# Attention block on one core: tiles 2 and 3 of the attention result turned by DMA, and later filling of the head groups' margins in DRAM

## The chip, the core and the metric

The kernel runs on one core of a Trainium2 chip. The engines are TensorE (PE in the tables; PEld is its weight load), VectorE (DVE), ScalarE (ACT), GpSimd (POOL) and SyncE (SP), whose queue issues nearly all DMAs. The metric is the time in device microseconds of one execution. The time before is 507.06 us, the median of three runs (505.41 to 508.73).

## The reference

One pre-norm block over S = 2048 rows of D = 512, one batch, in f32:

```python
h = x + attention(layernorm(x)) @ wo            # 32 heads of 16, W = 8 keys, dilation 2
#   q, k, v = layernorm(x) @ wqkv
#   row s sees rows s, s-2, ... s-14 (those below 0 masked), softmax over the 8
out = h + (relu(layernorm(h) @ w1 + b1) ** 2) @ w2 + b2     # w1: 512 x 1792
```

## The kernel before

**Tiling.** The 2048 rows are 16 tiles of 128. Four tiles form a group (`R = 4`), and attention works on pairs of tiles (`RI = 2`): pair s is tiles 2s and 2s+1, its result is `o_t[s]`. Each product is made of three fp32r matmuls per block (high times high, high times low, low times high), so every operand of a product is cast to a high part on ACT (line 152) and a low part, source minus high part, on DVE or POOL (line 155).

**Stages.** To about 64 us, tiles 0 to 3 are projected piece by piece, eight heads (one "gp" of four) at a time. Then tiles 4 to 15 are projected (`first_phase`), while DVE and POOL work on attention; the `wo` products of tiles 0 to 3 stand among these. From about 160 us three sub-blocks u = 0, 1, 2 run the MLP of one group of tiles beside the attention results and `wo` products of the next group; the MLP of the last group ends the program.

**Order.** The program order of each engine is fixed when the kernel is built. A clock of planned times, `now["pe"]` and `now["dve"]`, does it: work is put into slots with `at`, `midway` and `after`, and at the end of a slot `pump` emits attention steps on DVE as long as `now["dve"]` is below `now["pe"]`. Whatever is added to or left out of `now["pe"]` therefore moves the attention steps against the other work on DVE, POOL, ACT and SP. Every engine executes its list in order, so an instruction that waits holds all behind it.

**Attention.** One step multiplies q by a window of keys (line 339, `pr<-qp,k`), a reduction (line 373) gives logits, softmax follows, the weights are multiplied by a window of values (line 350, `pr<-ex,v`), and POOL adds the eight products up (line 407, `pr<-pr` and last `o<-pr`). q, k and v live in DRAM in `qkv_d`: ACT evacuates a projected piece to the buffer `y2`, which has two halves (lines 521 and 523), SP stores it (lines 497 and 500), and SP loads windows of k, v and q (lines 247 and 260). Each head group has a margin of eight rows in front of its second chain, filled by `store_halo` (line 487): two DMAs from DRAM to DRAM for each gp, emitted two slots after the store of that gp's first pair of tiles. They read rows that this store writes, so SP waits there until the store has landed.

**Turning the result.** The `wo` product needs `o_t` with features on the partitions. Tiles 4 to 15 (`OV`) go by DMA: `o_split` copies the 16-bit halves apart on ACT (line 616), `turn_dma` issues a DMA transpose on SP (line 620), `o_join` copies the halves together on ACT (line 625). Tiles 0 to 3 go through PE (`o_T`: four 128x128 transposes, line 201), at the half slots `OT = 4, 5, 10, 12`, with the `wo` products at `WO = 7, 9, 13, 15`. In both ways the high and low parts `oh` and `ol` (in one buffer `ohl` for the third tile of a group) are made after it. The buffers `row(...)` come from one pool of 15 that rotates. `h_add` (line 661, `h<-wo`) adds the residual on DVE and waits for the end of a tile's `wo` product.

Of the kernel before, what the change touches and what calls it, by code (L numbers as in the profile page):

```python
# [19 lines left out]
R = 4  # L20
RI = 2
# [9 lines left out]
LAG = 3  # L31
HALF = 2.6
AS = (8, 9, 12, 13)
OV = tuple(range(4, 16))
HV = (0,1,4,5,8,9,12,13)
SLOW = 1.01, 1.08, 1.05
DELAY = 3
# [21 lines left out]
def block_kernel(ctx, tc, x, wqkv, wo, w1, b1, w2, b2, out):  # L59
# [15 lines left out]
    def chain(e, g, c, r, ap):  # L75
        block = (e * 3 + c) * G + g
        return bass.AP(tensor=qkv_d.tensor, offset=qkv_d.offset + block * CS + r * GC, ap=ap)
# [35 lines left out]
    def at(delta, fn, *a):  # L113
        due.setdefault(now["slot"] + delta, []).append((fn, a))
# [115 lines left out]

    items = [(s, g0, 2) for g0 in range(0, G, 2) for s in range(RI)]
    items += [(s, g0, 4) for s in range(RI, NS) for g0 in range(0, G, 4)]
    stored = set()
    done = {s: 0 for s in range(NS)}
    o_t = {}

# [34 lines left out]
    def attention():  # L271
# [1 line left out]
        N = len(items)  # L273

        def ready(n):
            return n < N and all((items[n][0] // RI, (items[n][1] + j) // 2) in stored
                                 for j in range(0, items[n][2], 2))

        steps = [(n, j) for n in range(N) for j in range(items[n][2])]
        ks, vs, qs, qps, ex = {}, {}, {}, {}, {}  # L280
# [203 lines left out]
    def store_halo(gp):  # L484

        for g in (2 * gp, 2 * gp + 1):
            nc.sync.dma_start(chain(0, g, 2, 0, [[G * 3 * CS, 2], [GC, PAD], [1, GC]]),
                              chain(0, g, 2, PAD, [[0, 2], [0, PAD], [1, GC]]))

    def store(t, gp, c, y):  # L490

        b, r = divmod(t, 8)
        e, i = divmod(r, 4)
        pos = PAD + CH // 2 * b + i
        if c is None:
            for j in range(2):
                nc.sync.dma_start(chain(e, 2 * gp + j, 0, pos,
                                        [[R * GC, P], [G * CS, 3], [1, RI * GC]]), y[:, :, j])
        else:
            nc.sync.dma_start(chain(e, 0, c, pos, [[R * GC, P], [CS, G], [1, RI * GC]]), y)  # L500
        if t == 0:
            at(2, store_halo, gp)
        if i == R - RI:
            if c is None:
                stored.add((t // R, gp))
            elif c == 2:
                stored.update((t // R, gp) for gp in range(G // 2))
# [84 lines left out]
    def o_T(t):  # L592
        s, j = divmod(t, RI)
        pump(until=s)
        tr = transposes(o_t[s][:, j, :])
        if t % R == RI:

            ohl = att.tile([P, 2, KB, P], F32R, name="ohl", tag="o", bufs=3)
            oT[t] = ohl[:, 0], ohl[:, 1]
        else:  # L600
            oT[t] = row("oh", (P, KB, P), F32R), row("ol", (P, KB, P), F32R)
        at(0, hi_T, tr, [oT[t][0]])
        at(0, lo_T, tr, [oT[t][0]], [oT[t][1]])
# [30 lines left out]
    def o_join(t):  # L634
        turn_join(("o", t))
        tr = planes.pop(("o", t))
        if t % R == RI:
            ohl = att.tile([P, 2, KB, P], F32R, name="ohl", tag="o", bufs=3)
            oT[t] = ohl[:, 0], ohl[:, 1]
        else:  # L640
            oT[t] = row("oh", (P, KB, P), F32R), row("ol", (P, KB, P), F32R)
        hi_T(tr, [oT[t][0]])
        (at if t >= 12 else midway)(0, lo_T, tr, [oT[t][0]], [oT[t][1]])

    def h_split(t):
        turn_split(("h", t), hn.pop(t))
# [360 lines left out]
    def first_phase(t0):  # L1007
        def chores(m):
            if t0 + 3 < 16:
                if m in (0, 2):  # L1010
                    at(0, x_stats, t0 + 2 + m // 2)

                early = t0 == 12
                if m + early in ((4, 6) if t0 == R else (6, 7)):
                    at(0, x_norm, t0 + 2 + (m + early) // 7 if t0 > R else t0 + m // 2)
                if m in XT[early]:
                    x_T(t0 + 2 + XT[early].index(m))
            if t0 + 5 < 16 and m in (6, 9):
                at(0, load_x, t0 + 2 + m // 3)
            if jobs and m % 3 == 0:  # L1020
                at(0, weight_job)
            k = t0 // 2 * 12 - 72 + m
            if k == 19:
                dve(HOLD)
            for t in range(R):
                if k == OT[t]:
                    at(0, load_h, t)
                    o_T(t)
                if t in HV and k == HK[t][0]:
                    at(0, h_split, t)  # L1030
                    after(0, turn_dma, ("h", t))
                if t in HV and k == HK[t][1]:
                    at(0, turn_join, ("h", t))
                if k == WO[t]:
                    wo_product(t, (1, 3, 4, 6))
                    now["pe"] += 2.73
                if k == HT[t]:
                    (at(0, h_parts, t) if t in HV else h_T(t))
            if k in W2:
                at(0, load_w2, W2.index(k))  # L1040

        def half(m):
            end_slot(1.37)
            chores(m)

        for n in range(6):
            chores(2 * n)
            qkv_of(t0 + n % 2, n // 2, lambda: half(2 * n + 1))
            end_slot(1.37)
# [200 lines left out]
```

## Time and profile before

| | |
|---|---|
| three runs | 505.41, 507.06, 508.73 us |
| the profiled execution | 506.54 us, of which 504.7 us are the span of its instructions |
| mean granted TensorE clock | 0.999 |
| busy: PE, PEld | 497.3 us (99%), 421.1 us (83%) |
| busy: DVE, POOL, ACT | 380.5 us (75%), 356.4 us (71%), 304.2 us (60%) |
| DMA queue of SP | 101.61 MB, 68.8% of the 16 DMA engines' span |
| DMA share from 64 to 120 us, from 120 to 140 us | 0.94, 0.75 |
| PE transposes of `o` (tiles 0 to 3) | 16 of 272 ns, 2.4 us in all |

Times in rows are microseconds from the first instruction, unless a row says ns. A row of the timeline is: start, duration, engine, line, operation, output and inputs, shapes, count, and in brackets the idle time of the engine just before, with what ended it. Matmuls overlap, so PE's durations add up to more than the time between starts; differences of starts are used for PE. The busy shares are averages: what matters for a change is which engine ends the wait at its place.

### The profile page before, as it was taken

The numbers are of one execution on the slowest core, as the hardware profiler recorded it, in microseconds if no ns is written. First come the engines' busy times: TensorE is split into PE (matmuls) and PEld (weight loads), VectorE is DVE, ScalarE is ACT, GpSimd is POOL, SyncE is SP. The second block draws the span as 40 slices with busy tenths as digits, with TensorE's granted clock in tenths as the row PEclk, the third lists the DMA queues.
The fourth block names the chain that finished last, engine by engine and source line by source line (L and its number), as shares of the span: only waits on it lengthen the run. The fifth ranks groups of instructions, "written<-read, shape, count | busy, mean of one in ns | idle before, by whom it ended". The sixth has DMA issues, their size and how long they took to land.

```text
span 504.7 us, 7544 instructions
## 1 busy us (share of the span) xinstructions
PE 497.3 (99%) x2422; PEld 421.1 (83%) x2422; DVE 380.5 (75%) x512; ACT 304.2 (60%) x558; POOL 356.4 (71%) x434
## 2 busy tenths in 40 slices
PE   8999999999999999999999999999999999999997
PEld 7999778888888888888888888778888888998986
DVE  6479799999989999788879988998972147833233
ACT  4634677768346758378464567845566937666541
POOL 5714789896685999879777876896897464685610
PEclk9999999999999999999999999999999999999999
DMA  8678899999698999679576866867672372354112
GB/s 268 200 213 201 241 306 296 267 279 306 211 219 255 302 279 260 202 215 259 161 256 213 211 199 166 210 230 257 204 169 71 98 198 83 130 159 150 64 43 83
DMA packets 109359, 102.61 MB, mean 203 GB/s; under 512 B 29448, under 2 KB 77832, under 8 KB 109320
## 3 DMA queue, kind: packets, MB, share of 16 engines
q1 hardware_dynamic: 108376, 101.61, 68.8%
q10 hardware_dynamic: 944, 0.52, 0.3%
q8 instruction: 19, 0.31, 0.2%
q14 instruction: 20, 0.16, 0.1%
HBM read 72.65 MB, written 24.25 MB: 192 GB/s over the span
## 4 chain that ended last, share of the span: by engine, by line
PE 73%; POOL 5%; ACT 5%; DVE 3%; issue 2%; DMA 1%; SPq 0%; POOLq 0%; ACTq 0%
PE mm L228 35%; PE acc L895 23%; PE wo L228 7%; PE mm L818 6%; POOL pr L407 2%; PE tr L201 2%; ACT pl L616 1%; DVE pr L350 1%; DMA h<-h_d 1%; POOL o L407 1%; POOL rl L155 1%; ACT r L872 1%; POOL h L674 1%; ACT r L871 0%; ACT hn L196 0%
## 5 line engine op out<-in xcount | busy, mean ns | idle before, releaser
L407 POOL TENSOR_TENSOR pr<-pr 128x512 f32<-128x512 f32 (+1 forms) x128 | 133.9, 1046 | 34.2 <-DVE pr L350 28.8
L228 PE MATMUL mm<-big_l,w_h 128*128 128x512 f32 x336 | 88.5, 389 | 0.1
L350 DVE TENSOR_TENSOR pr<-ex,v 128x1024 f32<-128x1024 f32 x64 | 78.0, 1220 | 12.9 <-POOL o L407 7.9
L339 DVE TENSOR_TENSOR pr<-qp,k 128x1024 f32<-128x1024 f32 x64 | 76.8, 1201 | 7.8 <-ACT qp L268 7.2
L373 DVE TENSOR_REDUCE ex<-pr 128x64 f32<-128x1024 f32 x64 | 78.5, 1226 | 1.9
L228 PEld LDWEIGHTS mm<-big_l,w_h 128*128 128x128 f32 x336 | 63.0, 188 | 13.6 <-ACT qp L268 0.5
L155 POOL TENSOR_TENSOR rl<-r,rh 128x512 fp32r<-128x512 f32 x42 | 55.2, 1316 | 20.3 <-ACT rh L152 20.2
L228 PE MATMUL mm<-big_l,xh 128*128 128x512 f32 (+1 forms) x208 | 55.8, 378 | 0.0
L228 PE MATMUL mm<-big_h,xh 128*128 128x512 f32 (+1 forms) x208 | 53.7, 379 | 0.7 <-ACT xh L152 0.7
L228 PE MATMUL mm<-big_h,xl 128*128 128x512 f32 (+1 forms) x208 | 52.7, 375 | 0.8 <-DVE xl L155 0.8
L895 PE MATMUL acc<-big_l,rh 128*128 128x512 f32 x190 | 52.2, 390 | 0.0
L895 PE MATMUL acc<-big_h,rh 128*128 128x512 f32 x190 | 52.1, 391 | 0.0
L895 PE MATMUL acc<-big_h,rl 128*128 128x512 f32 x190 | 51.7, 389 | 0.0
L228 PE MATMUL mm<-big_l,w_l 128*128 128x512 f32 x168 | 44.9, 389 | 0.0
L228 PEld LDWEIGHTS mm<-big_h,xh 128*128 128x128 f32 x208 | 37.7, 188 | 7.6 <-ACT xh L152 1.8
L228 PEld LDWEIGHTS mm<-big_h,xl 128*128 128x128 f32 x208 | 38.2, 188 | 7.0 <-DVE xl L155 1.2
L895 PEld LDWEIGHTS acc<-big_h,rl 128*128 128x128 f32 x190 | 35.7, 188 | 7.5
L895 PEld LDWEIGHTS acc<-big_l,rh 128*128 128x128 f32 x190 | 35.5, 188 | 7.4
L228 PEld LDWEIGHTS mm<-big_l,xh 128*128 128x128 f32 x208 | 37.5, 188 | 4.9
L871 ACT ACTIVATE r<-mm,b_sb 128x512 f32<-128x512 f32 x42 | 28.8, 685 | 19.8 <-PE mm L228 19.8
L895 PEld LDWEIGHTS acc<-big_h,rh 128*128 128x128 f32 x190 | 34.9, 188 | 6.7
L228 PEld LDWEIGHTS mm<-big_l,w_l 128*128 128x128 f32 x168 | 31.5, 188 | 6.6
(167 smaller groups left out, 917.5 us busy)
## 6 DMA issues: line engine op xcount, KB each, us to landing
k<-qkv_d SPq DMA_DIRECT2D x48, 288.0 KB, 3.0
v<-qkv_d SPq DMA_DIRECT2D x48, 288.0 KB, 3.2
qkv_d<-y SPq DMA_DIRECT2D x18, 512.0 KB, 4.9
big_l<-w2l_d SPq DMA_DIRECT2D x24, 256.0 KB, 3.1
xt<-in_A_x_dram SPq DMA_DIRECT2D x16, 256.0 KB, 4.7
q<-qkv_d SPq DMA_DIRECT2D x32, 128.0 KB, 3.4
h<-in_A_x_dram SPq DMA_DIRECT2D x16, 256.0 KB, 3.7
h_d<-h SPq DMA_DIRECT2D x16, 256.0 KB, 3.2
```

The lines of the kernel that those rows point to most:

```text
L155: eng.tensor_tensor(out=dst, in0=src, in1=h, op=ALU.subtract)
L201: nc.tensor.transpose(tr[:, k, :], src[:, k * P:(k + 1) * P], ident)
L228: nc.tensor.matmul(ps, l(k), r(k), start=(n == 0), stop=(n == 3 * KB - 1))
L339: nc.vector.tensor_tensor(out=pr.rearrange("p i w h d -> p i w (h d)"), in0=qps["now"][:, j % 2].unsqueeze(2).to_broadcast([P, RI, W, GC]) ...
L350: nc.vector.tensor_tensor(out=p2, in1=vwin, op=ALU.mult, in0=e1[:, :, :, j * GH:(j + 1) * GH].unsqueeze(4).to_broadcast([P, RI, W, GH, DH]))
L373: nc.vector.tensor_reduce(out=lf[:, :, :, j * GH:(j + 1) * GH], in_=pr, axis=X, op=ALU.add)
L407: nc.gpsimd.tensor_tensor(out=dst, in0=p2[:, :, :w], in1=p2[:, :, w:2 * w], op=ALU.add)
L616: nc.scalar.copy(two_planes(planes[key][1]), halves_of(src))
L674: nc.gpsimd.tensor_tensor(out=h, in0=h, in1=b2_sb, op=ALU.add)
L818: nc.tensor.matmul(ps, sta[y][:, k], mov[x][:, k], start=(first and q == 0), stop=(last and q == len(terms) - 1), skip_group_check=True)
L871: nc.scalar.activation(r, ps, AF.Relu, bias=b1_sb[:, f:f + 1])
L895: nc.tensor.matmul(acc[j], l[:, j * P:(j + 1) * P], w[f], start=(first and n < len(js)), stop=(last and n >= len(terms) - len(js)))
```

## The change

`OV` now holds tiles 2 and 3 too: they are turned as tiles 4 to 15 are. `OK` gives the half slots: split at 6 and 8, join at 11 and 13; the transposes on PE at 10 and 12 are gone. The `wo` products stay at 13 and 15; for tiles in `OV` they take the term with the low part last. Second, `store_halo` is put four slots behind the store and no longer two (for the first gp it stays in the second slot, but behind what that slot holds already), and attention may start on a gp only when its margin has been issued (`padded`).

```diff
-OV = tuple(range(4, 16))
+OV = tuple(range(2, 16))
+OK = {2: (6, 11), 3: (8, 13)}
...
-            return n < N and all((items[n][0] // RI, (items[n][1] + j) // 2) in stored
-                                 for j in range(0, items[n][2], 2))
+            gps = [(items[n][1] + j) // 2 for j in range(0, items[n][2], 2)] if n < N else []
+            return n < N and all((items[n][0] // RI, gp) in stored and gp in padded
+                                 for gp in gps)
...
+        padded.add(gp)
...
         if t == 0:
-            at(2, store_halo, gp)
+            if gp:
+                at(4, store_halo, gp)
+            else:
+                at(2, at, 0, at, 0, store_halo, gp)
...
-        (at if t >= 12 else midway)(0, lo_T, tr, [oT[t][0]], [oT[t][1]])
+        (at if t >= 12 or t < R else midway)(0, lo_T, tr, [oT[t][0]], [oT[t][1]])
...
                 if k == OT[t]:
                     at(0, load_h, t)
-                    o_T(t)
+                    if t not in OV:
+                        o_T(t)
+                if t in OK and k == OK[t][0]:
+                    at(0, o_split, t)
+                    after(0, turn_dma, ("o", t))
+                if t in OK and k == OK[t][1]:
+                    at(0, o_join, t)
```

Line numbers of the changed kernel are larger by 1 to 6 for the same code (line 487 is 489 there, 497 is 500, 661 is 667).

The order on SP from the fifth store to the last margin, before:

```order
L497 DMA qkv_d<-y_90 128x3x128 x2
L260 DMA q<-qkv_d 128x2x128
L487 DMA qkv_d<-qkv_d 2x8x64 x2
L497 DMA qkv_d<-y_90 128x3x128 x4
L247 DMA k<-qkv_d 128x704
L260 DMA q<-qkv_d 128x2x128
L487 DMA qkv_d<-qkv_d 2x8x64 x2
L438 DMA xt<-in_A_x_dram 128x512
L497 DMA qkv_d<-y_90 128x3x128 x2
```

The same stretch with the change:

```order
L500 DMA qkv_d<-y_90 128x3x128 x2
L261 DMA q<-qkv_d 128x2x128
L500 DMA qkv_d<-y_90 128x3x128 x2
L489 DMA qkv_d<-qkv_d 2x8x64 x2
L500 DMA qkv_d<-y_90 128x3x128 x2
L248 DMA k<-qkv_d 128x704
L261 DMA q<-qkv_d 128x2x128
L440 DMA xt<-in_A_x_dram 128x512
L500 DMA qkv_d<-y_90 128x3x128 x2
```

The margin of the second gp (`qkv_d<-qkv_d`) stands one store later; that of the third has left this stretch and stands behind the load of `b_sb`; that of the fourth stands behind `raw<-in_A_wo_dram` and one more store, where it stood ahead of both.

ACT around the turning of tile 2, with the change (before, the three rows with `pl<-o` are not there and the cast of `ohl` reads `tr`, the result of PE):

```order
L622 COPY pl<-o 128x1024
L153 CAST xh<-tr 128x512
L269 COPY qp<-q 128x256
L529 COPY y_90<-mm 128x8x64
L153 CAST xh<-tr 128x512
L622 COPY pl<-o 128x1024
L153 CAST w_h<-raw 128x448
L529 COPY y_90<-mm 128x8x64
L197 ACTIVATE hn<-h,rs 128x512
L631 COPY pl<-o 128x1024
L153 CAST ohl<-pl 128x512
L153 CAST w_h<-raw 128x448
```

The splits of tiles 2 and 3 (line 622) and the join of tile 2 (line 631) are new; the join of tile 3 follows a little later, ahead of the cast of its `oh`. `hn<-h,rs` now stands ahead of the cast of `ohl`, where it stood behind it.

DVE in sub-block u = 0, around the residual additions of tiles 4 and 5, before:

```order
L373 TENSOR_REDUCE ex<-pr 128x16x4
L661 TENSOR_TENSOR h<-wo,h 128x512
L163 BN_STATS st<-h 128x6
L164 BN_AGGR mv<-st 128x2
L339 TENSOR_TENSOR pr<-qp,k 128x1024
L350 TENSOR_TENSOR pr<-ex,v 128x1024
L373 TENSOR_REDUCE ex<-pr 128x16x4
L155 TENSOR_TENSOR ol<-pl,oh 128x512
L350 TENSOR_TENSOR pr<-ex,v 128x1024
L661 TENSOR_TENSOR h<-wo,h 128x512
```

And with the change:

```order
L667 TENSOR_TENSOR h<-wo,h 128x512
L164 BN_STATS st<-h 128x6
L165 BN_AGGR mv<-st 128x2
L375 TENSOR_REDUCE ex<-pr 128x16x4
L341 TENSOR_TENSOR pr<-qp,k 128x1024
L352 TENSOR_TENSOR pr<-ex,v 128x1024
L156 TENSOR_TENSOR ol<-pl,oh 128x512
L375 TENSOR_REDUCE ex<-pr 128x16x4
L667 TENSOR_TENSOR h<-wo,h 128x512
L164 BN_STATS st<-h 128x6
L165 BN_AGGR mv<-st 128x2
L352 TENSOR_TENSOR pr<-ex,v 128x1024
```

One attention step that stood ahead of each `h<-wo,h` now stands behind it. The same has happened in u = 1 at tile 8: before, `ex<-pr`, `ol<-pl,oh`, `pr<-qp,k`, `h<-wo,h`, `pr<-ex,v`; now `ol<-pl,oh`, `ex<-pr`, `h<-wo,h`, `pr<-qp,k`, `pr<-ex,v`. The PE transposes that are left out no longer add their 2 times 0.44 us to `now["pe"]`.

More of the change, by code (lines that the diff above doesn't have):

```diff
@@ L232, in block_kernel @@
     items += [(s, g0, 4) for s in range(RI, NS) for g0 in range(0, G, 4)]
-    stored = set()
+    stored, padded = set(), set()
     done = {s: 0 for s in range(NS)}
```

## The prediction

> **What bounds the kernel now.** I read the share of each engine first, then PE's waits, then the places of those waits.
>
> ```profile
> span 504.7 us, 7544 instructions
> PE 497.3 (99%) x2422; PEld 421.1 (83%) x2422; DVE 380.5 (75%) x512; ACT 304.2 (60%) x558; POOL 356.4 (71%) x434
> PE wo L228 <- ACT ohl L152: 0.8, 1, 0.8
> PE mm L228 <- DVE xl L155: 0.8, 1, 0.8
> ```
>
> The first two lines are the head of the page, the others are from the table of PE's waits (total, times, longest). PE is without work for only 7.4 us of the span, so a gain has two sources: fewer matmuls, or one of those waits. The reverse weighs more: DVE, POOL and ACT have spare time on average, but each executes in order, and wherever one of them delivers late to PE, that time is lost in full. The profiled execution took 506.54 us; I add terms to that. It lies 0.5 us below the median of 507.06, less than the runs differ among themselves, so I forecast the median by the same number.
>
> **Term 1: the transposes on PE.** PE's timeline at tile 2:
>
> ```profile
> 134.99 0.60 PE L201 MATMUL tr<-ident,o 128*128 128x128 f32 x4
> 135.34 1.17 PE L228 MATMUL mm<-big_h,xh 128*128 128x512 f32 x4
> 136.35 1.08 PE L228 MATMUL mm<-big_l,xh 128*128 128x512 f32 x4
> 137.27 1.07 PE L228 MATMUL mm<-big_h,xl 128*128 128x512 f32 x4
> ```
>
> Four matmuls of 512 columns take 137.27 - 136.35 = 0.92 us; with the transposes ahead of them, 136.35 - 134.99 = 1.36. So a turning costs PE 0.44 us net, and PE has no wait here: two of them gone are **-0.9**, with little doubt.
>
> What takes their place is paid elsewhere. The groups of instructions, split by shape, and the list of DMAs (median us to landing):
>
> ```profile
> L616 ACT COPY pl<-o 128x1024 uint16<-128x1024 uint16 x12 | 12.5, 1043 | 8.3 <-POOL o L407 8.3
> L625 ACT COPY pl<-o 128x1024 uint16<-128x1024 uint16 x12 | 14.0, 1170 | 1.4 <-DMA o<-pl 1.3
> L155 DVE TENSOR_TENSOR ohl<-pl,ohl 128x512 fp32r<-128x512 f32 x3 | 4.0, 1325 | 7.7 <-ACT ohl L152 7.7
> L155 DVE TENSOR_TENSOR ohl<-tr,ohl 128x512 fp32r<-128x512 f32 x1 | 0.7, 657 | 0.0
> L155 DVE TENSOR_TENSOR ol<-pl,oh 128x512 fp32r<-128x512 f32 x9 | 7.9, 883 | 0.0
> L155 DVE TENSOR_TENSOR ol<-tr,oh 128x512 fp32r<-128x512 f32 x3 | 2.1, 688 | 2.4 <-ACT oh L152 2.4
> o<-pl SPq DMA_TRANSPOSE x12, 3.8
> ```
>
> ACT gets two splits and two joins, 2 x (1.04 + 1.17) = 4.4 us, and DVE's low parts cost (1.33 - 0.66) + (0.88 - 0.69) = 0.9 us more. The landing of 3.8 us does not count. ACT's row ahead of the new split is
>
> ```profile
> 123.80 0.82 ACT L196 ACTIVATE xt<-xt,rs 128x512 f32<-128x512 f32 x1
> ```
>
> so tile 2's split ends near 125.7, and its join, five half slots of about 2.3 us later, comes near 136.4. SP gets two issues, ahead of a k load and of a weight load; the loads run two steps ahead and DMA has a share of 0.75 here (table above), so I take nothing, with 0 to 0.7 us as bounds (one issue held back).
>
> The low parts read `tr` from PSUM before, and now two operands in SBUF. The rows show the effect: 657 ns against 1325, 688 against 883. The Trainium skill (SBUF — State Buffer, "SBUF: two separate sides") says that a VectorE operation with two SBUF inputs and a GpSimd operation that reads SBUF lock each other out for a whole instruction. By that rule the difference is chance by chance up to one POOL operation, and not a fixed price; the means of the rows agree with it, and the second rival below is what it would do at its worst.
>
> **Term 2: the margins.** SP, ACT, DVE and PE, one after the other:
>
> ```profile
> 37.42 1.23 SPq L487 DMA_DIRECT2D qkv_d<-qkv_d  x2
> 49.63 1.24 SPq L487 DMA_DIRECT2D qkv_d<-qkv_d  x2
> 51.86 0.89 SPq L497 DMA_DIRECT2D qkv_d<-y  x2
> 50.22 0.59 ACT L523 COPY y<-mm 128x512 f32<-128x512 f32 x1 [3.26 <-DMA qkv_d<-y]
> 56.13 0.58 ACT L523 COPY y<-mm 128x512 f32<-128x512 f32 x1 [1.22 <-DMA qkv_d<-y]
> 57.63 0.29 DVE L362 TENSOR_REDUCE sm<-ex 128x16 f32<-128x128 f32 x1 [2.40 <-ACT ex L396]
> 63.10 0.68 DVE L155 TENSOR_TENSOR xl<-tr,xh 128x512 fp32r<-128x512 f32 x1
> 63.83 0.96 PE L228 MATMUL mm<-big_h,xl 128*128 128x512 f32 x3 [0.77 <-DVE xl L155]
> ```
>
> The fourth gp's margin waits on SP to 49.63, and behind it stands the store of 51.86, whose landing ACT waits for at 56.13. ACT executes in order, so the softmax behind that evacuation is late, DVE waits 2.40 us for it, and the low part at 63.10 makes PE wait 0.77. With the margins behind the stores, this store goes out as soon as its data are there, some 4 us earlier, and ACT loses at least the 1.22. DVE has no other wait between 57.63 and 63.10 that could take up 0.77 us. **-0.77**; bounds -0.8 and 0 (the softmax found late for another reason). SP now waits for the last margin with v loads behind it, but from about 48 rather than 49.63.
>
> **Term 3: the start of u = 0.** The joins come late on an ACT that DVE waits for anyway:
>
> ```profile
> 140.44 0.69 DVE L155 TENSOR_TENSOR ol<-tr,oh 128x512 fp32r<-128x512 f32 x1 [1.74 <-ACT oh L152]
> 161.39 0.74 DVE L155 TENSOR_TENSOR big_l<-tr,big_l 128x256 fp32r<-128x256 f32 x2
> 163.21 1.98 PE L228 MATMUL mm<-big_l,w_h 128*128 128x512 f32 x8
> ```
>
> Following ACT's new list (evacuation, `hn`, join, cast of `ohl`) I get `ohl` ready near 138.2, where DVE took it at 136.91, and tile 3's `oh` near 142.6. DVE, almost without other gaps to 160, is then about 1.1 us later. Against this, one reduction of 1.2 us now stands behind the first MLP low parts and not ahead. Their end stays near 162.1; PE, 0.9 us earlier by term 1, wants the last at 163.21 - 0.9 = 162.3. I take **+0.1**, bounds 0 and 0.7.
>
> **Term 4: tile 6 in u = 0.** With 0.88 less on PE's planned clock, each attention step falls behind the residual addition that it stood ahead of (order of DVE, above). That addition waits for PE:
>
> ```profile
> 205.15 0.69 DVE L661 TENSOR_TENSOR h<-wo,h 128x512 f32<-128x512 f32 x1 [1.63 <-PE wo L228]
> 209.11 2.44 POOL L407 TENSOR_TENSOR pr<-pr 128x512 f32<-128x512 f32 x2 [1.62 <-DVE pr L350]
> 218.57 1.05 ACT L616 COPY pl<-o 128x1024 uint16<-128x1024 uint16 x1 [1.73 <-POOL o L407]
> 228.49 0.62 ACT L152 CAST ohl<-pl 128x512 fp32r<-128x512 f32 x1
> 229.43 0.84 PE L228 MATMUL wo<-wo_h,ohl 128*128 128x512 f32 x3
> ```
>
> The reduction ran in PE's shadow before 205.15; now it is executed after it, so the next product with v, and POOL's sum that waits for it at 209.11, are 1.15 us later. POOL has no gap to the last `o`, ACT waits for that to split tile 6 at 218.57, and ACT has no gap from there to the cast that ends at 229.11. PE takes it at 229.43: slack 0.32. All this hangs on PE's own clock through the `wo` at 205.15, so term 1 changes nothing. 1.15 - 0.32 gives **+0.8**; bounds 0 (the softmax or a copy elsewhere gives the step back) and 1.2.
>
> **Term 5: tile 10 in u = 1.** The same at tile 8:
>
> ```profile
> 293.40 0.69 DVE L661 TENSOR_TENSOR h<-wo,h 128x512 f32<-128x512 f32 x1 [0.61 <-PE wo L228]
> 299.29 2.48 POOL L407 TENSOR_TENSOR pr<-pr 128x512 f32<-128x512 f32 x2 [1.34 <-DVE pr L350]
> 307.37 1.05 ACT L616 COPY pl<-o 128x1024 uint16<-128x1024 uint16 x1 [2.07 <-POOL o L407]
> 317.95 0.62 ACT L152 CAST ohl<-pl 128x512 fp32r<-128x512 f32 x1
> 318.62 1.21 PE L228 MATMUL wo<-wo_h,ohl 128*128 128x512 f32 x4 [0.78 <-ACT ohl L152]
> ```
>
> Here the multiplication with k, 1.2 us, falls behind the wait. The sum at 299.29 comes 1.2 to 1.3 us later, POOL then has no gap to the `o` at 307.34, ACT none from there to 318.57, and PE waits already. The stall of 0.78 becomes about 2.0: **+1.2**, bounds -0.8 (the order helps and the stall goes) and 1.5.
>
> **Term 6: u = 2.**
>
> ```profile
> 396.89 0.62 ACT L152 CAST ohl<-pl 128x512 fp32r<-128x512 f32 x1
> 401.74 1.07 PE L228 MATMUL wo<-wo_h,ohl 128*128 128x512 f32 x4
> ```
>
> The cast is 4.2 us ahead of PE, more than one step: **0**.
>
> **The sum.** -0.9 - 0.77 + 0.1 + 0.8 + 1.2 + 0 = +0.43, so 506.54 + 0.43 = **507.0 us**. The change gives PE 1.7 us and takes about 2 back through the order of DVE. A difference of 1% (5 us) is about what a measurement of this kernel can tell from no change, so this is no change that a few runs would show.
>
> **The rivals.**
>
> *The gains stay.* The step's delay is absorbed: DVE, POOL and ACT wait in all for 1.6 to 2.1 us on that chain (rows of terms 4 and 5), and if POOL's or ACT's list is favourable, the split goes out as before. For it: in both chains the waiting engine idles just ahead of the split. Against it: it idles because the one before it is late, which the step makes worse. Price: terms 3 to 5 fall away: 506.54 - 1.67 = 504.9 us. If the stall of 0.78 goes too, 504.1. Chance 0.25.
>
> *VectorE becomes the bound at the start of u = 0* (slower). Mechanism: the two new low parts read two SBUF operands and are held by POOL each time. For `ohl<-pl` the trace has one of 1.81 us:
>
> ```profile
> 318.60 1.81 DVE L155 TENSOR_TENSOR ohl<-pl,ohl 128x512 fp32r<-128x512 f32 x1 [0.58 <-ACT ohl L152]
> ```
>
> If both low parts take that long, DVE loses (1.81 - 1.33) + (1.81 - 0.88) = 1.4 us more than in term 3, and if `oh` is also late by one held copy of 1.05 us on ACT, about 2.5. It decides as soon as the last MLP low part ends after 162.3 on PE's clock; beyond that PE loses it one to one, since DVE and PE stay busy with no gap there. 507.0 + 2.5 = 509.5 us. Against it: the mean of the group is 883 and 1325 ns, and that is in term 3. Chance 0.2.
>
> *The margins do nothing for PE.* ACT's evacuation at 56.13 is freed, but the softmax is late by another load that SP now holds behind the last margin; the stall at 63.83 stays. 507.0 + 0.77 = 507.8 us. Speaks against it that SP's waits in this stretch all get shorter. Chance 0.1.
>
> There is a rule against the first half of the change as such: the Trainium skill (VectorE: DVE Perf Modes, "The three transpose paths" and "Rules for kernel authors") gives 390 ns for a 128x128 transpose on TensorE and 1309 by DMA, and advises TensorE where PSUM will do as its target. By latency the rule would keep PE; as the landing is hidden here (11 us from split to join) it changes no term, and the sum by it would only lose the -0.9, 507.9.
>
> **How the numbers follow.** Forecast 0.45, gains stay 0.25, VectorE bound 0.2, margins idle 0.1. The likeliest case gives the prediction, 507.0. The range reaches from the full gain with some scatter of runs, 504.2, to the slower rival, 509.6; each side leaves out about one in ten (the bounds of terms 3 to 5 at their worst together give 506.54 - 1.67 + 3.4 = 508.3, inside). Over 1% faster would need below 502, more than PE's waits and both gains give together: 0.03. Over 1% slower, beyond 512, needs the slower rival twice over: 0.07.
>
> **What would show it.** Right: 8 fewer transposes, no wait of PE near 63, waits of PE for `ohl` of about 0.8 us at tile 6 (near 228) and of about 2 at tile 10 (near 317). Term 3 is wrong if PE waits near 161 for a `big_l` low part. Terms 4 and 5 are wrong if the splits of tiles 6 and 10 lie no later against PE than before. All of it is wrong if PE shows waits of over 3 us in sum at places not named here, above all for k, v or the evacuation of projections between 120 and 160.

## The result and the profile after

The changed kernel takes **508.79 us** (median of 22 runs, 507.18 to 510.97), the kernel before 507.0 us beside it on the same chip (22 runs, 505.41 to 508.73). The ratio is 1.0038, with an interval of 1.0029 to 1.0046: slower by 0.4%. The forecast was 507.0 us, which is no change, in a range of 504.2 to 509.6. The time lies in the range, but the 1.8 us that the change costs were not forecast.

The profiled execution took 508.45 us. Of its page the head, and of the table of PE's waits (total, times, longest):

```profile
span 506.6 us, 7539 instructions
PE 497.0 (98%) x2414; PEld 420.5 (83%) x2414; DVE 377.9 (75%) x512; ACT 308.9 (61%) x562; POOL 356.2 (70%) x434
PE wo L229 <- ACT ohl L153: 2.7, 2, 1.9
PE mm L229 <- DVE xl L156: 0.8, 1, 0.8
PE mm L229 <- ACT r L877: 0.5, 1, 0.5
PE mm L229 <- DVE big_l L156: 0.2, 1, 0.2
```

PE has the 8 transposes less (2422 to 2414) and ACT the 4 copies more. The wait for `xl` that the margins were to take away is still there, the wait for `ohl` went from 0.8 to 2.7 us, and two waits are new. PE's timeline shows where they lie:

```profile
63.79 0.73 PE L229 MATMUL mm<-big_h,xl 128*128 128x512 f32 x2 [0.77 <-DVE xl L156]
160.71 1.16 PE L229 MATMUL mm<-big_l,w_h 128*128 128x512 f32 x4 [0.18 <-DVE big_l L156]
169.64 1.19 PE L229 MATMUL mm<-big_l,w_h 128*128 128x512 f32 x4 [0.50 <-ACT r L877]
230.50 0.73 PE L229 MATMUL wo<-wo_h,ohl 128*128 128x512 f32 x2 [0.72 <-ACT ohl L153]
321.05 0.73 PE L229 MATMUL wo<-wo_h,ohl 128*128 128x512 f32 x2 [1.93 <-ACT ohl L153]
```

**Stretches.** To place the time I cut each span at instructions of PE that all kernels have (a transpose of `xt` or `hn`, a `wo` product) and took the differences of their starts in PE's timeline. In the table "start" ends at the fourth transpose of `xt`; "margins" is the stretch from 59 to 74 us, "turning" the one from 129 to 156 (the first transpose of `hn`), "u=0" from the next transpose of `hn`, 3.2 us later, to the first `wo` product of tile 4, "tile 6" and "tile 10" the stretches between the `wo` products of tiles 5 and 6, and 9 and 10, "u=2" from the end of u = 1 to the `wo` product of tile 12. The stretches left out differ by 0.25 us at most, but for two in e8_all_early, which the text on it names.

```
                  start  margins  turning    u=0  tile 6  tile 10    u=2   span
before            14.42    15.15    27.29  42.68   17.22    18.17  43.00  504.7
after             14.38    15.16    26.33  43.88   18.11    19.32  42.62  506.6
e1_halo_only      14.39    14.58    27.30  42.65   17.23    18.18  43.01  504.1
e2_halo_pinned    14.41    14.09    27.30  42.65   17.23    18.16  43.01  503.6
e3_turn_only      15.84    14.55    26.31  43.92   18.21    19.37  42.63  507.7
e4_order_only     14.14    14.63    27.30  42.64   18.10    19.32  42.63  505.7
e5_turn_paid      14.55    16.21    26.32  43.57   17.41    18.18  43.01  506.3
e6_all_paid       14.85    14.88    26.31  43.57   17.37    18.18  43.04  505.2
e7_all_pinned     14.81    14.08    26.32  43.53   17.41    18.18  43.04  504.3
e8_all_early      14.32    14.08    26.32  46.13   17.23    17.22  42.68  508.0
e9_one_ahead      15.81    14.07    27.29  42.63   17.23    17.22  43.59  504.5
e10_joins_early   14.36    14.09    26.33  44.31   17.23    18.20  43.61  504.8
e11_best          14.38    14.09    26.33  44.49   17.23    17.22  43.62  503.9
e12_one_turn      14.49    14.08    26.62  42.63   17.23    18.18  43.01  503.0
```

After against before: turning -0.96, u=0 +1.20, tile 6 +0.89 (and +0.14 right behind), tile 10 +1.15, u=2 -0.38, margins nothing; that makes +2.0 of the 1.9 us between the spans, and the medians differ by 1.8. Between kernels with the same code in a stretch its time agrees to some 0.05 us, 0.10 at most (tile 6 in after and e3_turn_only), except in "start" and "margins": before, e3, e4 and e5 have the same code there, and one execution of each took 14.55 to 16.21 us in "margins". So I compare stretches, and the ratios only as a second witness. A wait costs PE more than its idle time: where an old wait grew, at tile 10, the loss is the growth (0.78 to 1.93, 1.15), but at tile 6 a new wait of 0.72 cost 0.89, and in u=0 two new ones of 0.18 and 0.50 cost 1.20, about 0.2 to 0.3 more for each new wait.

### The profile page after: what moved, and what is told of

Same layout as the page of the kernel before. It is cut to its first block, busy times and chain, and to the rows that moved or that the text cites. A ratio compares the mean times of both kernels' runs of the same rounds, so it can differ in the third digit from the quotient of the medians.

```text
span 506.6 us, 7539 instructions
## 1 busy us (share of the span) xinstructions
PE 497.0 (98%) x2414; PEld 420.5 (83%) x2414; DVE 377.9 (75%) x512; ACT 308.9 (61%) x562; POOL 356.2 (70%) x434
## 4 chain that ended last, share of the span: by engine, by line
PE 47%; POOL 8%; ACT 6%; DVE 4%; issue 2%; DMA 1%; SPq 0%; POOLq 0%; ACTq 0%; DVEq 0%
PE acc L901 21%; PE mm L229 15%; PE mm L824 6%; PE wo L229 4%; POOL pr L409 3%; POOL rl L156 1%; ACT pl L622 1%; DMA raw<-in_B_w_dram 1%; ACT r L877 1%; DVE pr L341 1%; POOL o L409 1%; DVE pr L352 1%; POOL h L680 1%; ACT r L878 1%; ACT hn L197 1%
```

## The experiments

Ratios are against the kernel before on the same chip.

**The margins alone.** The edit is the diff's part on `store_halo` and `padded`; tiles 2 and 3 stay on PE.

> Only the margins are put later; tiles 2 and 3 stay on PE. Theory: ACT's evacuation near 56 comes 1.6 us earlier, but the multiplication with k on DVE that started at 54.00 now waits for POOL to about 56.4, because the build gives it the buffer that POOL still reads; the wait of PE near 63.8 stays at 0.77 and the profiled execution takes 506.5 us as before (median within 0.3 of the kernel before). Rival (the buffer plays no part, the gain was lost through the turned tiles): the wait near 63.8 is gone, 505.7 us.

Measured: 506.27 us (12 runs), ratio 0.9995 (0.9985 to 1.0005): no difference. Its margins stretch has 14.58 where before has 15.15, but with unchanged margins it was also 14.55 and 14.63 in two other kernels below. The theory's wait of DVE for POOL is there; its other half, that PE's wait near 63.8 stays at 0.77, did not hold in this execution: POOL was 0.6 us earlier than in the change, and PE's product began at 63.17, without a listed wait. DVE in this stretch, first before, then the margins alone, then the whole change:

```profile
54.00 1.22 DVE L339 TENSOR_TENSOR pr<-qp,k 128x1024 f32<-128x1024 f32 x1 [0.19 <-ACT qp L268]
```

```profile
55.83 1.22 DVE L340 TENSOR_TENSOR pr<-qp,k 128x1024 f32<-128x1024 f32 x1 [1.69 <-POOL o L408]
```

```profile
56.45 1.22 DVE L341 TENSOR_TENSOR pr<-qp,k 128x1024 f32<-128x1024 f32 x1 [3.04 <-POOL o L409]
57.59 0.28 DVE L364 TENSOR_REDUCE sm<-ex 128x16 f32<-128x128 f32 x1
```

ACT and POOL of the whole change at the same place:

```profile
54.54 0.58 ACT L529 COPY y<-mm 128x512 f32<-128x512 f32 x1
55.73 0.26 ACT L398 ACTIVATE ex<-ex 128x128 f32<-128x128 f32 x1
```

```profile
55.96 0.46 POOL L409 TENSOR_TENSOR o<-pr 128x128 f32<-128x128 f32 x1
```

What the prediction followed did happen: the evacuation started at 54.54, where it stood at 56.13 before, and the softmax behind it ended at 55.99. But DVE did not use it. Its multiplication `pr<-qp,k`, which started at 54.00 before, now waited until POOL had finished reading a product at 56.42, and the reduction `sm<-ex` behind it started at 57.59, where it was at 57.63 before. One wait took the place of the other, to 0.04 us. The order of DVE's list had not changed here; its waits had. These are two multiplications with k that stand four instructions apart on DVE (59 and 63 are their places in its list, and the brackets name the engines they wait for), before and after:

```
59 L339 TENSOR_TENSOR pr<-qp,k 128x1024 [waits Activation_49]
63 L339 TENSOR_TENSOR pr<-qp,k 128x1024 [waits Pool_49]

59 L341 TENSOR_TENSOR pr<-qp,k 128x1024 [waits Activation_49,Pool_49]
63 L341 TENSOR_TENSOR pr<-qp,k 128x1024
```

The products `pr` share three buffers that the build hands out. With the margins moved, the first of these two products was given a buffer that POOL still reads, and the second one that DVE's own reduction frees; before it was the other way round.

**The same with the buffers named.** To test this I gave the `pr` buffers by name, in the sequence of before. The few other tiles that share these three buffers are named too; the order of DVE's list is that of the margins alone. The first of the edited lines:

```diff
-pr = att.tile([P, RI, W, GH, DH], F32, name="pr", bufs=3)
+pr = att.tile([P, RI, W, GH, DH], F32, name="pr", tag="pr" + next(turns), bufs=1)
```

> As e1, but each product buffer is named by hand in the sequence that the kernel before had, so the multiplication with k does not wait for POOL. Theory: it starts at about 54.1, the softmax is there at 55.7, PE's wait near 63.8 is gone: 0.8 us under the kernel before, profiled 505.7 us. Rival (POOL's sum or the loads are late in any case): PE's wait stays, 506.5 us.

Measured: 505.57 us (10 runs), ratio 0.9982 (0.9967 to 0.9997). DVE in this stretch:

```profile
53.51 1.22 DVE L342 TENSOR_TENSOR pr<-qp,k 128x1024 f32<-128x1024 f32 x1
55.05 0.29 DVE L365 TENSOR_REDUCE sm<-ex 128x16 f32<-128x128 f32 x1 [0.32 <-ACT ex L399]
```

No wait for POOL, the softmax's reduction is 2.6 us earlier than in before, and PE has no wait near 63. The stretch takes 14.09 us; it took 14.07 to 14.09 in each of the seven kernels with moved margins and named buffers, 14.58 to 15.16 with moved margins and the build's choice (three kernels), and 14.55 to 16.21 with the margins of before (four). So the margins are worth 0.5 to 2.1 us when the buffer stays, and the buffer took it away in the change.

**The turning alone.** The diff's part on `OV`, `OK` and the copies; margins as before.

> Only tiles 2 and 3 are turned by DMA; the margins stay where they were. Theory (the order on DVE costs the time): PE waits 0.7 for ohl near 230, 1.9 near 320, 0.5 for r near 169, as with the whole change; -0.9 + 0.7 + 1.1 + 0.5 + 0.2 = +1.6, profiled 508.1 us. Rival (the later margins cost it, by the DMA queue): at most 505.7 us.

Measured: 510.49 us (6 runs), ratio 1.0078 (1.0059 to 1.0097). The stretches from turning on repeat those of the whole change (26.31, 43.92, 18.21, 19.37), and its waits too. So the loss belongs to this half. The median is 3.7 us above before, of which these stretches explain 2.2; the profiled run shows a start that was 1.4 us longer, and the other runs aren't seen.

**The order alone.** The kernel before, turning on PE, but with the 0.44 taken off the planned clock at tiles 2 and 3, so that POOL's list is that of the change, and DVE's too, but for the low part of tile 3, which stands ahead of a product with v and not behind it:

```diff
+                    if t in (2, 3):
+                        now["pe"] -= 0.44
```

> The kernel before, with tiles 2 and 3 on PE, but 0.44 taken off PE's planned clock at each of their two transposes, so that DVE and POOL get exactly the order of the changed kernel. Theory (the order alone costs the time): PE waits near 169, 230 and 320 as with the change, 506.5 + 0.7 + 1.1 + 0.5 = 508.8 us or a little more. Rival (ACT's four copies, the two transposes on SP and the DMA load cost it): 506.5 us, PE waits only 0.8 near 319.

Measured: 509.12 us (6 runs), ratio 1.0061 (1.0043 to 1.0079); the profiled run, at 507.49, is the lowest of them. PE's timeline:

```profile
229.47 1.19 PE L228 MATMUL wo<-wo_h,ohl 128*128 128x512 f32 x4 [0.71 <-ACT ohl L152]
320.03 1.19 PE L228 MATMUL wo<-wo_h,ohl 128*128 128x512 f32 x4 [1.93 <-ACT ohl L152]
```

Without a single DMA turning more, tile 6 and tile 10 lose what they lose in the change (18.10, 19.32). So terms 4 and 5 are the shifted step alone. The stretch u=0 loses nothing (42.64), though a wait near 169 was expected: its loss needs the turning.

**The turning with its order paid back.** The turning alone, and where PE's transposes are left out the planned clock still gets their 0.44; DVE's list is then that of before, but for the same low part:

```diff
                     if t not in OV:
                         o_T(t)
+                    else:
+                        now["pe"] += 0.44
```

> Only tiles 2 and 3 are turned by DMA, and PE's planned clock still gets 0.44 at the two places of the transposes, so that DVE and POOL keep the order of the kernel before. Theory: the waits near 169 and 230 are gone, the one near 320 is back at 0.8; the 0.9 us of the transposes stay, profiled 505.6 us. Rival (PE, now 0.9 us earlier, runs into weights and low parts that are not earlier, at the start of u = 0): 0.5 to 1.2 us are lost there again, 506.1 to 506.8 us.

Measured: 507.36 us (12 runs), ratio 1.0001 (0.9984 to 1.0018). Tile 6 and tile 10 are back (17.41, 18.18), turning has its 0.97 less, and u=0 has 0.89 more, by one wait, as the rival said:

```profile
162.41 1.15 PE L229 MATMUL mm<-big_l,w_h 128*128 128x512 f32 x4 [0.62 <-ACT y L526]
```

The bracket names an evacuation on ACT; what this product does wait for is worked out at the end of this section. So the turning by itself, without the shifted order, is worth -0.97 + 0.89 + 0.19 (tile 6): about nothing.

**The whole change, paid back; and with the buffers named.** Two kernels: the change with the same two lines, and that one with `pr` named as above.

> The whole change with PE's planned clock paid as in e5. Theory: as e5, and as e1 showed for the margins with the changed buffers, 0 to 0.5 us less: 505.1 to 505.6 us. Rival (margins and turned tiles disturb each other on SP): over 506.5 us.

Measured: 507.35 us (12 runs), ratio 1.0006 (0.9985 to 1.0028). The time is the rival's, but its cause doesn't show: the stretches are those of the turning paid back, and the theory had counted on the 0.97 that u=0 takes back.

> As e6, with the product buffers named by hand as in e2. Theory: the gains add up, 1.0 of e2 and 0.9 of the transposes: 504.6 us; it beats both kernels. Rival (the start of u = 0 gives the 0.9 back): 505.5 us.

Measured: 506.06 us (12 runs), ratio 0.9972 (0.9957 to 0.9986). With the order and the buffer of before, the change gains about 0.3%; its stretches differ from those of the margins with named buffers only by -0.98 in turning, +0.88 in u=0 and +0.18 at tile 6, so its gain is that of the margins. The start of u = 0 gives the 0.9 back, as the rival said.

**The step pushed the other way.** The last kernel with 0.88 in place of 0.44, so that each step comes earlier than in before:

> As e7, but 0.88 instead of 0.44 is added at the two places, so that attention steps move one step ahead of the order before. Theory (each step ahead of a residual addition takes its time out of PE's wait): PE's wait for tile 10's ohl near 317, 0.8 in all kernels with the old order, gets smaller or goes, 503.8 to 504.3 us. Rival (the step now stands ahead of the MLP's low parts at 161): a wait of about 1 us there, 505.5 us.

Measured: 508.22 us (12 runs), ratio 1.0027 (1.0004 to 1.005). Tile 10 loses its wait (17.22), as the theory said, and the rival's wait near 161 came too; neither had the rest. u=0 takes 46.13, with PE waiting there three times:

```profile
160.31 1.15 PE L229 MATMUL mm<-big_l,w_h 128*128 128x512 f32 x4 [0.90 <-DVE big_l L156]
162.81 2.14 PE L229 MATMUL mm<-big_l,w_h 128*128 128x512 f32 x8 [0.45 <-DVE big_l L156]
170.77 1.20 PE L229 MATMUL mm<-big_l,w_h 128*128 128x512 f32 x4 [1.28 <-ACT r L882]
340.57 0.66 PE L202 MATMUL tr<-ident,hn 128*128 128x128 f32 x4 [2.24 <-ACT hn L197]
```

The fourth, at the end of u = 1, lies in a stretch left out of the table (4.23 us there, 1.82 in before; the other is the one behind tile 10's, 17.07 for 16.54). So the sign of the step isn't a rule: each stall has its own place.

**One step earlier in u = 1 only.** The margins with named buffers, turning on PE, and the planned clock 0.88 ahead from slot 0 to slot 12 of u = 1:

```diff
+            if u == 1 and p in (0, 12):
+                now["pe"] += 0.88 if p == 0 else -0.88
```

> As e2 (margins later, buffers named by hand, tiles 2 and 3 on PE), and only in the first part of u = 1 PE's planned clock is 0.88 ahead, taken back behind the split of tile 10. In DVE's order three pairs change: each of the residual additions of tiles 8 and 9 falls behind one multiplication with v, and the low part of tile 9 behind a reduction. Theory (the place of one step against an addition that waits for PE sets when POOL, ACT and then PE get on): the opposite move to that of the change, so PE's wait of 0.8 for tile 10's ohl goes, the stretch from tile 9's product to tile 10's takes 17.3 us in place of 18.2, 502.7 us. Rival (tile 10's wait has another source, such as the landing of its transpose): 18.2 us stay, 503.6 us.

Measured: 504.98 us (12 runs, 504.63 to 506.65), ratio 0.9963 (0.9949 to 0.9976): the fastest kernel of this study that computes the whole, ahead of before and of the change. The wait at tile 10 is gone (17.22 for 18.16), and a wait that was not expected stands at the start of u = 2 (+0.58), so that 0.58 of the 0.94 won is lost again:

```profile
338.87 1.15 PE L228 MATMUL mm<-big_l,w_h 128*128 128x512 f32 x4 [0.71 <-DVE big_l L155]
```

**The joins one half slot earlier.** The whole change, paid and with named buffers, and the joins at 10 and 12:

```diff
-OK = {2: (6, 11), 3: (8, 13)}
+OK = {2: (6, 10), 3: (8, 12)}
```

> As e7, but the joins of tiles 2 and 3 stand one half slot earlier (10 and 12). Theory (the joins and casts on ACT make DVE late, by its waits of 0.6 and 1.4 us for the casts near 137 and 142): DVE's waits shrink, its low parts at 160 end up to 1 us earlier, and the start of u = 0 takes 42.7 to 43.0 us in place of 43.5. Rival (PE is earlier than DVE there by the 0.97 of the transposes alone, whatever the joins do): 43.5 us stay.

Measured: 506.42 us (12 runs), ratio 0.9991 (0.9978 to 1.0004). The stretch u=0 got worse, 44.31, against what either theory expected, and u=2 is 0.57 longer, with a wait of 0.7 for `big_l`. DVE's low parts of the two turned tiles, and the product with v beside the second, with the joins as in the change and then one half slot earlier:

```profile
137.53 0.69 DVE L156 TENSOR_TENSOR ohl<-pl,ohl 128x512 fp32r<-128x512 f32 x1 [0.62 <-ACT ohl L153]
139.27 1.22 DVE L354 TENSOR_TENSOR pr<-ex,v 128x1024 f32<-128x1024 f32 x1
141.91 0.69 DVE L156 TENSOR_TENSOR ol<-pl,oh 128x512 fp32r<-128x512 f32 x1 [1.42 <-issue]
```

```profile
136.40 0.69 DVE L156 TENSOR_TENSOR ohl<-pl,ohl 128x512 fp32r<-128x512 f32 x1
140.79 0.69 DVE L156 TENSOR_TENSOR ol<-pl,oh 128x512 fp32r<-128x512 f32 x1 [2.56 <-ACT oh L153]
141.40 1.22 DVE L354 TENSOR_TENSOR pr<-ex,v 128x1024 f32<-128x1024 f32 x1
```

DVE lost the wait for `ohl` and got one of 2.56 us for `oh`. The edit had changed DVE's order as well, at this one place: the low part of `oh` now stands ahead of a product with v of 1.2 us, and no longer behind it. So DVE came to it before ACT had made `oh`, and these waits together grew from 2.04 to 2.56 us. Why PE lost so much by it, the last part of this section shows.

**Both.** The last kernel with the step of u = 1 put ahead:

> e9 and e10 together on the whole change: margins later, buffers named by hand, tiles 2 and 3 by DMA with PE's planned clock paid and the joins earlier, 0.88 ahead in the first part of u = 1. Theory: the gains add up, 0.9 less than e10 in tile 10's stretch; it beats the kernel before by 2.5 to 3.5 us. Rival: the turned tiles give back what they gain, no better than e9.

Measured: 505.93 us (12 runs), ratio 0.998 (0.9967 to 0.9992). Tile 10 has no wait, u=0 takes 44.49; it is no better than the step alone with turning on PE, as the rival said.

**What u=0 waits for.** These kernels give a rule for the start of u = 0. As a mark I take the first `h<-wo` on DVE after 129 us. In before, the mark is at 130.82, and the pair of low parts that PE's first MLP product needs (`big_l<-tr`) and that product are

```profile
159.60 0.74 DVE L155 TENSOR_TENSOR big_l<-tr,big_l 128x256 fp32r<-128x256 f32 x2
161.38 1.09 PE L228 MATMUL mm<-big_l,w_h 128*128 128x512 f32 x4
```

In the whole change, the mark and the pair are

```profile
130.77 0.68 DVE L667 TENSOR_TENSOR h<-wo,h 128x512 f32<-128x512 f32 x1
159.82 0.74 DVE L156 TENSOR_TENSOR big_l<-tr,big_l 128x256 fp32r<-128x256 f32 x2
```

The same places in the other kernels; where PE waits, its product starts 0.89 us after the pair starts. This holds in e7 and e10 too, where the profile's bracket names a work of ACT for the wait; in the program this product has no wait for that work, but one for the pair.

```
                  DVE's pair after the mark    PE's product after the mark    PE's wait
before                    28.78                       30.56                      -
after                     29.05                       29.94                     0.18
e3_turn_only              29.06                       29.95                     0.20
e7_all_pinned             29.47                       30.36                     0.62
e8_all_early              29.75                       30.64                     0.90
e10_joins_early           30.06                       30.95                     1.20
```

Take the wait off, and PE reaches the product 29.74 to 29.76 us after the mark in all five turned kernels, 0.8 us earlier than before. In before PE could have started at 28.78 + 0.89 = 29.67 and did at 30.56: 0.89 us to spare (the same number by chance). The turning uses this up from both sides: PE is 0.8 earlier, and DVE later by 0.27 to 1.28. The wait is what goes beyond 0.89.

DVE's delay has two parts. One is its waits for the joins and casts on ACT. The other lies in the four low parts of `hn` just ahead of the pair, in before and in e7:

```profile
156.74 2.94 DVE L155 TENSOR_TENSOR big_l<-pl,big_l 128x256 fp32r<-128x256 f32 x4 [0.65 <-ACT big_l L152]
156.35 3.35 DVE L156 TENSOR_TENSOR big_l<-pl,big_l 128x256 fp32r<-128x256 f32 x4
```

After the mark they start at 25.92 and 26.20 and take 0.41 us more in e7, so of the 0.69 that DVE is later there, 0.28 are waits ahead of them. Their single times in e7 go from 0.43 to 1.51 us; the longest ends at 159.70, 0.28 behind an addition of POOL (`h<-h,b_sb`, 157.95 to 159.42) that ran beside it, and in before the longest, 1.52 us, ends 0.29 behind the same addition. DVE thus seems to be held by POOL here, which no run tried alone. In the change itself 0.08 of the 0.27 lie ahead of these low parts and 0.19 in them; from e7 to e10 all 0.59 lie ahead of them.

To test the rule I took away ACT's four copies and kept PE early: the margins with named buffers, turning on PE with one transpose for each of tiles 2 and 3 in place of four, the other three blocks of the result read from the first. Three quarters of that turning are left out, so the result of these tiles isn't the reference's; the other engines do the same work in the same order.

```diff
-        tr = transposes(o_t[s][:, j, :])
+        if t in (2, 3):
+            tr = turn["tr"].tile("tr").rearrange("p (k c) -> p k c", k=KB)
+            nc.tensor.transpose(tr[:, 0, :], o_t[s][:, j, 0:P], ident)
+            now["pe"] += 0.44
+            tr = tr[:, 0:1, :].to_broadcast([P, KB, P])
+        else:
+            tr = transposes(o_t[s][:, j, :])
```

> This is the kernel with the margins moved and the product buffers named by hand, turning tiles 2 and 3 on PE, but with one 128x128 transpose for each tile instead of four; the other three blocks of the result are read from the same block, so three quarters of the turning of these tiles are left out. ACT, DVE, POOL and SP have the same instructions in the same order. PE is thus about 0.7 us earlier after the turning, and no other engine has work added. Theory (DVE's own clock): at the start of u = 0 PE wants DVE's first pair of low parts and had 0.89 us to spare there; the turning by DMA makes PE earlier and DVE later, and the stall is what goes beyond the spare time. Without DVE's delay the 0.7 us stay inside it: DVE's low part begins 28.8 us after its addition of tile 0's residual, as before, PE has no wait for it, the stretch at the start of u = 0 stays within 42.6 to 42.8 us, the turning stretch is 26.5 to 26.7, and the span 502.7 to 503.1 apart from the start of the program (ratio about 0.996 to 0.997). Rival (all that PE wins ahead of u = 0 is lost there, since weights, evacuations and DVE come when they come): the stretch at the start of u = 0 is 43.2 to 43.5 us with a wait of 0.4 us or more, and the time is that of the kernel with four transposes (ratio about 0.998).

Measured: 505.3 us (10 runs), before 507.86 beside it, ratio 0.9958 (0.9943 to 0.9972); span 503.0. Turning takes 26.62 (-0.68), and u=0 42.63, with no wait there:

```profile
158.32 0.74 DVE L155 TENSOR_TENSOR big_l<-tr,big_l 128x256 fp32r<-128x256 f32 x2
```

```profile
159.72 1.07 PE L228 MATMUL mm<-big_l,w_h 128*128 128x512 f32 x4
```

PE starts 1.40 us after DVE's pair, 0.5 more than the 0.89 it needs. DVE's pair even comes 0.29 earlier after the mark than in before (28.49), as `hn` is turned and cast earlier; at before's 28.78 there would still be 0.2 to spare. So the 0.68 us won on PE ahead of u = 0 are kept when DVE isn't made later; the rival, that whatever PE wins is lost there, falls.

## Why the prediction was wrong in size, point by point

**The base.** The sum was +0.43 on the profiled 506.54, and the result, 507.0, is also the median before (507.06): a loss in the sum became no change in the forecast. Profile against profile the change took +1.9 (506.54 to 508.45). Nor is 1% the least that a measurement can tell here: 22 runs on each side gave 0.29% to 0.46%.

**Term 1, transposes, -0.9: right.** Turning is 0.96 us shorter, and in each turned kernel 0.96 to 0.98. ACT was read well too: the join of tile 2 came at 136.34 (forecast near 136.4, though 125.7 and five times 2.3 make 137.2), and `ohl` and `oh` were ready at 138.15 and 142.48 (138.2 and 142.6).

**Term 2, margins, -0.77: failed.** The step that failed is "DVE has no other wait between 57.63 and 63.10 that could take up 0.77 us". ACT was freed as predicted, but DVE's multiplication ahead of the reduction got a buffer that POOL reads. I had looked for another wait behind the stall and not ahead of it, and at the order of the instructions but not at what each of them waits for; the list of waits shows it before any run (59 and 63 above). The third rival gave 507.8 for "margins do nothing for PE", with the right outcome and another cause (loads behind the last margin). The size was also that of one execution: the stretch varies by 1.7 us among kernels with the old margins.

**Term 3, start of u = 0, +0.1: failed in size; it is +1.20.** The step that failed is "PE, 0.9 us earlier by term 1, wants the last at 163.21 - 0.9 = 162.3". DVE's side of it was near: I had 1.1 us of delay and 1.2 back by the moved reduction, and the last low part ends at 162.36 for 162.13. But PE's first MLP product, 1.8 us ahead of that row, already needs a first pair, with 0.89 us to spare, of which term 1 itself takes 0.8 and DVE's delay at this pair 0.27. The first wait is 0.18, for a `big_l` low part near 161, the very sign named for this term. The second, 0.50 for `r` at 169.64, comes from a queue I hadn't followed. ACT and SP after, then before:

```profile
168.38 0.62 ACT L153 CAST big_h<-raw 128x512 fp32r<-128x512 f32 x1 [2.63 <-DMA raw<-in_B_w_dram]
163.51 0.32 SPq L248 DMA_DIRECT2D k<-qkv_d  x1
164.36 0.46 SPq L1065 DMA_DIRECT2D raw<-in_B_w_dram  x1
```

```profile
168.15 0.62 ACT L152 CAST big_h<-raw 128x512 fp32r<-128x512 f32 x1 [1.82 <-DMA raw<-in_B_w_dram]
161.50 0.32 SPq L247 DMA_DIRECT2D k<-qkv_d  x1
163.66 0.42 SPq L1053 DMA_DIRECT2D raw<-in_B_w_dram  x1
```

SP issued the weights' load 0.70 us later, right behind a load of k that is 2.01 us later; ACT's cast, ahead of `r` in its list, waited for it and was 0.23 later, while PE had begun the MLP 0.67 us earlier (160.71 against 161.38, the mark plus 30.56). That load of k is late by the order: after the mark of u = 0 it is issued at 30.68 in before, 32.36 with the order alone, 32.74 in the change and 31.37 with the order paid back (e7). That it follows a multiplication that moved on DVE is read from the order of the lists. In e7 the weights' load goes out as late after the mark (33.54 us for 33.59 in the change), and PE has no wait for `r` there; so the late issue alone doesn't make this wait, and its cause stays open in part. The rest of the 1.20 is what PE loses beyond each idle time, about 0.25 twice.

**Term 4, tile 6, +0.8: right** (+0.89, a wait of 0.72, at 230.50). **Term 5, tile 10, +1.2: right** (+1.15, the wait of 0.78 became 1.93). Mechanism and size are shown by the order alone. "The splits lie later" held as well: ACT's split of tile 6 went from 218.57 to 219.92, that of tile 10 from 307.37 to 309.82, each 1.17 us later against PE's product of the tile before:

```profile
219.92 1.05 ACT L622 COPY pl<-o 128x1024 uint16<-128x1024 uint16 x1 [1.74 <-POOL o L409]
309.82 1.05 ACT L622 COPY pl<-o 128x1024 uint16<-128x1024 uint16 x1 [2.88 <-POOL o L409]
```

**Term 6, u = 2, 0: off by 0.38.** The order alone makes the start of u = 2 0.38 shorter as well (42.63), so the shifted step helps there. Most of it lies at PE's first MLP product of u = 2, which starts 2.08 us behind the transpose of `hn` in before and 1.82 in the change; the table of waits lists neither, and so I had nothing to go by.

**The rivals.** *The gains stay* fell: the step's delay came through in full. *VectorE becomes the bound through operands in SBUF* fell as it was put, though the time lay near: the two new low parts took 0.69 us each, as much as from PSUM:

```profile
138.19 0.69 DVE L156 TENSOR_TENSOR ohl<-pl,ohl 128x512 fp32r<-128x512 f32 x1 [0.63 <-ACT ohl L153]
142.57 0.69 DVE L156 TENSOR_TENSOR ol<-pl,oh 128x512 fp32r<-128x512 f32 x1 [1.42 <-issue]
```

At these two DVE was late by waiting, and not by being held. For the first the row names ACT; for the second it names nothing, but ACT's cast of `oh` ended at 142.48, 0.09 ahead of the start. The rule of the Trainium skill (SBUF — State Buffer, "SBUF: two separate sides") that was weighed there thus had no effect at these two places. The low parts of `hn` ahead of u = 0 (0.43 to 1.51 us, above) fit it, in before too, and elsewhere in the same profile low parts such as the new ones do take longer:

```profile
L156 DVE TENSOR_TENSOR ol<-pl,oh 128x512 fp32r<-128x512 f32 x10 | 8.3, 827 | 1.4 <-issue 1.4
L156 DVE TENSOR_TENSOR ohl<-pl,ohl 128x512 fp32r<-128x512 f32 x4 | 4.2, 1058 | 9.3 <-ACT ohl L153 9.3
```

The other rule of the Trainium skill, TensorE for a transpose where PSUM will do (VectorE: DVE Perf Modes, "The three transpose paths" and "Rules for kernel authors"; its times there are for bf16, the transposes here are f32), is not contradicted: with the order paid back the DMA transpose gained nothing (ratio 1.0001), though by another road than latency. The landing stayed hidden, as neither join waited for it; but DVE was later, in part by the copies on ACT that a DMA transpose brings, and that took the 0.96 us back.

The sum of +0.43 missed two terms, 0.77 and 1.10, less 0.38 of term 6. That gives +1.9, as the two profiles show.

## What to carry to other kernels

Where PE is busy 98% of the time, work taken off PE is kept only as far as the next stage's first operand is ready: set each win against the spare time of the first instruction that needs another engine, not the last. When a kernel's order comes from planned clocks and its buffers from rotating pools, compare the waits of each instruction as well as the order; a moved DMA changed which of three buffers a product got, and a wait of 3 us came of it. When a planner's cost is removed together with the work, try the kernel with the cost still charged: here that alone separates the work's own worth (about nothing) from the order's (1.8 us in e4_order_only's stretches).

## What the runs showed of the hardware

The start of the program varies from run to run: the fourth transpose of `xt` comes at 14.14 to 15.84 us, with the same instructions ahead of it. The first products on PE, in before and in the turning alone:

```profile
7.02 1.27 PE L228 MATMUL mm<-big_h,xh 128*128 128x384 f32 x4 [0.70 <-ACT xh L152]
8.13 0.86 PE L228 MATMUL mm<-big_h,xl 128*128 128x384 f32 x4
```

```profile
7.20 1.65 PE L229 MATMUL mm<-big_h,xh 128*128 128x384 f32 x4 [0.68 <-ACT xh L153]
8.65 1.49 PE L229 MATMUL mm<-big_h,xl 128*128 128x384 f32 x4
```

The same four matmuls take 1.27 or 1.65 us, the next four 0.86 or 1.49; from the third to the fourth transpose of `xt` both kernels take 2.8 us again. The granted clock reads 1.00 from 5 to 14 us in both profiles, so that column doesn't show it, and the cause stays open. A start of up to 1.7 us is a third of a per cent of this kernel, as much as the change makes: single profiled times can't rank such kernels, while most stretches between fixed instructions agree to some 0.05 us.
